# Storing a 128-row tile of the result as one transfer of two 64-row blocks, in a fused linear-attention and max-of-three feed-forward kernel

## The chip, the cores and the metric

The kernel runs on one core of one Trainium2 chip. A core has five engines with a queue of instructions each: TensorE (PE; its weight loads are listed apart as PEld), VectorE (DVE), ScalarE (ACT), GpSimd (POOL) and SyncE (SP), which here only issues transfers. Sixteen DMA engines carry the transfers that SP, ACT and POOL issue. The metric is the device time of one execution in microseconds (us); lower is better. Before the change the median of three runs was 283.24 us (282.25 to 283.63).

## What is computed

Batch 8, 8 heads, 576 tokens, head size 64. An attention with exponential features comes first; its output, 4608 rows of 512, goes through a feed-forward layer that takes the largest of three projections.

```python
def phi(x):
    proj = np.einsum('bhsd,df->bhsf', x, w_phi)             # 64 -> 128 features
    proj = proj - np.max(np.abs(proj), axis=-1, keepdims=True)
    return np.concatenate([np.exp(proj), np.exp(-proj)], axis=-1)
q_p, k_p = phi(q), phi(k)
kv = np.einsum('bhsf,bhsd->bhfd', k_p, v)
z = np.sum(k_p, axis=2)
num = np.einsum('bhsf,bhfd->bhsd', q_p, kv)
den = np.einsum('bhsf,bhf->bhs', q_p, z)[..., None] + 1e-06
x = (num / den)               # -> rows of (batch, token), 512 columns of (head, d)
h = np.maximum(np.maximum(x @ w1, x @ w2), x @ w3)          # 512 -> 768
out = h @ w_out                                             # 768 -> 512, float32
```

## The kernel before

**Tokens.** The 576 tokens of a head are loaded as 64 groups of nine (`c=NT`, `NT = 9`), so that 64 partitions hold one head and a partition reads 9 x 64 floats that lie together in DRAM. Token `9 i + c` is column `c` of partition `i`. Two heads share the 128 partitions. So in everything behind it the tokens of a batch stand in the order (c, i): first the 64 tokens with c = 0, then the 64 with c = 1, and so on.

**Units.** The attention works in 16 units (`attention`, four heads each, two units a batch): loads of q, k, v in float32 into `raw` buffers of 576 KB (eight of them); a cast to bf16 on POOL (`qk_bf`); a transpose to `qkT` (by TensorE for the first units, from unit 4 on by DMA on SP, L524); projections `psq` and `psk`; exponentials of k on ACT and maxima on DVE; the row maxima of q, turned on TensorE and put into row 64 of `qkT` by a transfer of 18 rows of 128 (`mT`, L582, on SP or ACT); the projections `psm` with their exponentials `Eq`; the products `kvps` and `psn`; and the division into `x_sb`. A second transpose by DMA on SP (`xT`, L703; by TensorE for the first two units) makes of `x_sb` the operand of the feed-forward layer.

**Chunks.** The feed-forward layer works in nine chunks (`chunk`). Chunk b = 0 to 7 holds the first 512 tokens of batch b in the order (c, i), that is c = 0 to 7; chunk 8 holds the tokens with c = 8 of all eight batches. A chunk multiplies by w2 - w1 and w3 - w1 (`ups`, L848), takes the maxima into `hT` on ACT and DVE, and adds x @ (w1 @ w_out) (L879) and `hT` @ w_out (L884) in PSUM. Chunks 0 to 4 copy each tile of 128 rows from PSUM to an `osb` buffer (four of them, `OSB`) and store it (L899). Chunks 5 to 8 (`FAST`) do this last product by Strassen's scheme of seven products of half size (`fast`, `fps`, L795), add up the tiles on DVE in two `raw` buffers, `low` and `high`, and store from there (L827).

**Stores.** A tile `tt` of a chunk b < 8 holds the 128 rows with c = 2 tt and c = 2 tt + 1. In the result, row `b * 576 + 9 i + c`, the 64 rows of one c stand 9 rows apart, and the two blocks of 64 start one row apart. `out_rows(tt)` gives a list of pairs (block of `out`, partitions of the tile), and the store issues one transfer for each. The chunk of the last tokens, b = 8, stores rows that stand 9 apart all through, in one transfer of 128 rows a tile, two tiles from SP and two from ACT.

**Order.** All instructions stand in a fixed order: `PLAN` lists each step with its engine, its start in the plan and its buffer, and every engine takes its steps in that order. SP's queue holds, mixed, the loads of `raw`, the transposes to `qkT` and `xT`, most of the `mT` transfers and all the stores of chunks 0 to 7. An engine waits at the step whose inputs or buffers aren't ready, with all that stands behind it. Transfers from SP and ACT take eight semaphores in turn; an issue waits until the transfer that last had its semaphore is done. The cost that a store has in the plan (`0.6 * n_out`) bears neither on the order, which `PLAN` fixes, nor on anything that is placed by it.

Of the kernel before, what the change touches and what calls it, by code (L numbers as in the profile page):

```python
# [19 lines left out]
P = 128  # L20
# [4 lines left out]
ST = S - SM  # L25
# [276 lines left out]
def kernel(  # L302
# [101 lines left out]
    def x_of(b):  # L404
        return xT[:, b % HELD]
# [311 lines left out]
    def t_nodes():  # L717
        for at, (n, c0) in enumerate(((2, 0), (2, 2), (1, 4))):
            def part(i, n=n, at=at):
                return t_end[:, i, :].unsqueeze(1) if at == 2 else xT[:, HELD + at, i, 0:DM].rearrange("p (c n) -> p c n", c=2)  # L720

            def quarter(r, w, n=n, c0=c0):
                m = slice(w * HF, (w + 1) * HF)
                return line_w[:, 2 * r:2 * r + 2, m] if c0 == 0 else wout_bf[:, 3 * r + c0 - 2:3 * r + c0 - 2 + n, m]
            pairs = [lambda q=quarter, p=part: (q(0, 1), q(0, 0)), lambda q=quarter, p=part: (q(1, 1), p(0)),
                     lambda q=quarter, p=part: (q(1, 1), q(0, 1)), lambda q=quarter, p=part: (q(1, 0), p(1))]
            need = [lines, [w_nodes[3]], [w_nodes[3]] + turned + diffs[0] + diffs[1]][at]
            made = []
            for i in range(4):
                def combine(i=i, pairs=pairs, part=part):  # L730
                    a, b = pairs[i]()
                    nc.gpsimd.tensor_tensor(part(i), a, b, ALU.subtract)
                n_ = node("tw", 0, {"POOL": 0.14 + 0.53 * n}, combine, need + [made[i - 1 - (i == 3)]] if i in (1, 3) else need, [])
                made.append(n_)
            t_made.extend(made)
# [220 lines left out]
    for b in range(B):  # L956
        if b == FAST[0]:
            t_nodes()
        rows = out[b * S:(b + 1) * S, :].rearrange("(i c) n -> c i n", c=NT)
        chunk(b, units[2 * b]["done"] + units[2 * b + 1]["done"], lambda ct, b=b: x_of(b)[:, ct, 0:SM],  # L960
              lambda ct, tt, b=b: x_of(b)[:, ct, tt * P:(tt + 1) * P],
              lambda tt, rows=rows: [(rows[2 * tt + i], slice(i * ST, (i + 1) * ST)) for i in range(2)], 2)
    lasts = []
    for b in range(B):
        lasts.append(node("C", 2 * b + 1, {"POOL": 0.4}, lambda b=b: nc.gpsimd.tensor_copy(
# [45 lines left out]
```

## Time and profile before

| | |
|---|---|
| median of 3 runs | 283.24 us |
| the profiled execution | 282.29 us |
| its span, first to last instruction | 280.5 us |
| granted TensorE clock, mean | 0.996 |
| HBM read and written | 34.64 MB and 9.44 MB |
| packets of DMA | 68050, of them 48746 under 512 B |

The span is shorter than the time by 1.8 us, which lie before the first and after the last instruction. A busy share is that of the whole span. The DMA rows give, for equal slices of the span or of a window, the busy share of the 16 DMA engines in tenths and the rate in GB/s. A row of a DMA queue has its number, kind, packets, MB, and the time that its packets took as a share of 16 engines in the window; q1 is SP's queue, q10 that of ACT. A row of the windows has the stretch in us, its length, the busy time of each engine with the count of its instructions, the granted clock, the share of DMA, and GB/s. In the chain of work that ended last, each row has a start, a duration and what held the path then. "SPq" is SP's sequencer: a row of it in the order of time has start, duration, line and transfer, and its durations are those of issuing, not of moving data.

### The profile page before, as it was taken

The page shows a single profiled execution, that of the slowest core. Times are in us where ns is not written, and L with a number is a line of the kernel's source. Part 1 is how long each engine was busy: PE and PEld are TensorE (multiplying, and loading weights), DVE is VectorE, ACT ScalarE, POOL GpSimd, SP SyncE. Part 2 cuts the span into 40 slices and gives each one's busy share as a digit, 9 for nine tenths or more (in the row PEclk, how much of TensorE's full clock was granted, in tenths as well). Part 3 has the DMA queues.
Part 4 walks back from the last instruction along what each step waited for, and adds up shares of the span by engine and source line. Part 5 has one row for each costly group of instructions (what it writes and reads, how often), then busy time and mean ns, then how long its engine had stood idle before and what let it go on. Part 6 is the DMA issues. An engine that isn't in the chain of part 4 may idle for free.

```text
span 280.5 us, 8829 instructions
## 1 busy us (share of the span) xinstructions
PE 270.9 (97%) x3663; PEld 164.1 (58%) x3663; DVE 224.0 (80%) x466; ACT 191.3 (68%) x439; POOL 168.5 (60%) x147
## 2 busy tenths in 40 slices
PE   8899999999999999999999999999999999999991
PEld 3566774465546555564556456565485589444881
DVE  4899899988869997889898878897589565756292
ACT  3799997798879988898684699887654860112000
POOL 8075787839444764570768079267875892927910
PEclk9999999999999999999999999999999999999998
DMA  7999999997999997799899729984232108245037
GB/s 212 234 211 320 266 224 197 384 277 139 287 382 245 197 313 251 193 204 227 240 263 156 194 49 261 202 201 89 51 78 49 40 18 118 55 95 116 0 89 212
DMA packets 68050, 51.46 MB, mean 183 GB/s; under 512 B 48746, under 2 KB 52650, under 8 KB 68010
## 3 DMA queue, kind: packets, MB, share of 16 engines
q1 hardware_dynamic: 63561, 45.41, 66.2%
q0 software_dynamic: 4000, 4.92, 10.3%
q8 instruction: 28, 0.46, 0.6%
q10 hardware_dynamic: 449, 0.57, 0.6%
q14 instruction: 12, 0.10, 0.1%
HBM read 34.64 MB, written 9.44 MB: 157 GB/s over the span
## 4 chain that ended last, share of the span: by engine, by line
PE 78%; DMA 9%; DVE 6%; ACT 3%; issue 1%; POOL 1%; DVEq 0%; POOLq 0%; ACTq 0%
PE ups L848 33%; PE fps L795 8%; PE ops L884 7%; PE psn L673 5%; PE kvps L655 5%; PE ops L879 5%; PE psq L547 5%; PE psm L626 5%; DMA qk_bf<-in_k_dram 3%; DMA qkT<-qk_bf 3%; DMA qkT<-mT 3%; ACT Eq L639 2%; DVE raw L802 2%; PE pm L950 2%; PE tps L509 1%; DVE mqp L566 1%
## 5 line engine op out<-in xcount | busy, mean ns | idle before, releaser
L601 POOL TENSOR_TENSOR vab<-raw,em 128x1152 bf16<-128x1152 f32 (+1 forms) x36 | 68.1, 1906 | 69.4 <-ACT em L597 55.1
L560 ACT ACTIVATE Ek<-psk 128x512 bf16<-128x512 f32 (+1 forms) x160 | 82.2, 568 | 13.8 <-PE psk L547 10.0
L848 PE MATMUL ups<-xT,w_bf 128*128 128x512 bf16 x384 | 90.8, 379 | 0.0
L639 ACT ACTIVATE Eq<-psm 128x512 bf16<-128x512 f32 (+1 forms) x160 | 79.4, 571 | 10.4 <-PE psm L626 9.6
L848 PEld LDWEIGHTS <-w_bf 128*128 128x128 bf16 x432 | 41.0, 98 | 46.4
L566 DVE TENSOR_REDUCE mqp<-psq 128x4 bf16<-128x512 f32 (+1 forms) x80 | 49.2, 634 | 8.4 <-PE psk L547 5.7
L566 DVE TENSOR_REDUCE mk<-psk 128x4 f32<-128x512 f32 (+1 forms) x80 | 48.9, 630 | 1.1 <-ACT Ek L560 0.5
L855 DVE TENSOR_TENSOR hT<-hT,ups 128x512 bf16<-128x512 bf16 x54 | 36.2, 684 | 16.8 <-PE ups L848 13.9
L857 ACT ACTIVATE hT<-ups 128x512 bf16<-128x512 f32 x28 | 16.6, 606 | 30.1 <-PE ups L848 30.0
L680 DVE TENSOR_TENSOR x_sb<-psn,rden 128x320 bf16<-128x320 f32 x64 | 31.5, 492 | 2.2
L492 POOL CAST qk_bf<-raw 128x1152 bf16<-128x1152 f32 x24 | 27.2, 1148 | 5.8 <-DMA qkT<-qk_bf 3.5
L673 PEld LDWEIGHTS <-Eq 128*128 128x128 bf16 x640 | 24.7, 97 | 7.5 <-ACT Eq L639 0.7
L884 PE MATMUL ops<-wout_bf,hT 128*128 128x512 bf16 x120 | 29.1, 379 | 0.0
L673 PE MATMUL psn<-kv_sb,Eq 128*128 128x65 bf16 x640 | 26.8, 194 | 0.5 <-ACT Eq L639 0.5
L547 PE MATMUL psq<-w,qkT 64*128 64x128 bf16 x288 | 24.5, 217 | 1.0 <-DMA qkT<-qk_bf 0.6
L547 PE MATMUL psk<-w,qkT 64*128 64x128 bf16 x288 | 24.1, 217 | 0.2
L547 PEld LDWEIGHTS <-qkT 64*128 64x128 bf16 x576 | 16.6, 94 | 12.7 <-issue 8.9
L626 PE MATMUL psm<-qkT,wphi_m 128*128 128x512 bf16 (+1 forms) x70 | 22.3, 359 | 0.5 <-DMA qkT<-mT 0.3
L879 PE MATMUL ops<-xT 128*128 128x512 bf16 x80 | 20.6, 380 | 0.0
L859 DVE TENSOR_SCALAR hT<-ups 128x512 bf16<-128x512 f32 x26 | 17.5, 684 | 3.8 <-PE ups L848 3.6
L655 PE MATMUL kvps<-vab,Ek 64*128 64x65 bf16 x1152 | 20.2, 190 | 0.0
L655 PEld LDWEIGHTS <-Ek 64*128 64x128 bf16 x1152 | 18.8, 94 | 2.3 <-DVE mk L566 0.4
(97 smaller groups left out, 333.8 us busy)
## 6 DMA issues: line engine op xcount, KB each, us to landing
raw<-in_v_dram SPq DMA_DIRECT2D x16, 576.0 KB
raw<-in_q_dram SPq DMA_DIRECT2D x12, 576.0 KB
raw<-in_k_dram SPq DMA_DIRECT2D x12, 576.0 KB
out_dram<-osb SPq DMA_DIRECT2D x40, 128.0 KB
out_dram<-raw SPq DMA_DIRECT2D x24, 128.0 KB
w_bf<-in_moe_w_dram POOLq DMA_DIRECT2D x3, 768.0 KB, 9.4
qk_bf<-in_q_dram POOLq DMA_DIRECT2D x3, 288.0 KB, 8.2
qk_bf<-in_k_dram POOLq DMA_DIRECT2D x3, 288.0 KB, 9.3
```

The lines of the kernel that those rows point to most:

```text
L547: nc.tensor.matmul(ps()[:, i, :], lhsT=cols[r, :], rhs=w2[r, c, :], start=True, stop=True)
L560: nc.scalar.activation(Ek[s]()[:, tiles_of(t0, n), :], of(1), EXP, scale=1.0 - 2.0 * s)
L566: nc.vector.tensor_reduce((mq, mk)[c]()[:, tiles_of(t0, n)], of(c), AXX, ALU.max, apply_absolute_value=True)
L601: (nc.vector if n_.eng == "DVE" else nc.gpsimd).tensor_tensor(vab()[:, g, t0:t1, 0:D], vb()[:, t0:t1, :], em()[:, g, t0:t1].unsqueeze(2).t ...
L626: nc.tensor.matmul(psm()[:, 0:w], lhsT=wphi_m, rhs=rhs, start=True, stop=True)
L639: nc.scalar.activation(Eqb()[s][:, cols], psm()[:, 0:w], EXP, scale=1.0 - 2.0 * s)
L655: nc.tensor.matmul(kvps[ab]()[:, t // NT, g, :], lhsT=Ek[g]()[r, t, :], rhs=vab()[r, g, t, :], start=(t + g == 0), stop=(t == UT - 1 and g ...
L673: nc.tensor.matmul(psn()[:, c, :], lhsT=Eqb()[g][:, t0:t0 + P], rhs=kv()[:, pr, ab, g, :], start=(g == 0), stop=(g == 1))
L848: nc.tensor.matmul(ups(), lhsT=w_bf[i + 1][:, ct, j * P:(j + 1) * P], rhs=tokens_of(ct), start=(ct == 0), stop=(ct == CT - 1))
L855: nc.vector.tensor_tensor(hT()[:, j, :], hT()[:, j, :], ups(), ALU.max)
L879: nc.tensor.matmul(ops_()[:, 0:width], lhsT=tile_of(ct, tt), rhs=line_w[:, ct, cols], start=(ct == 0), stop=False)
L884: nc.tensor.matmul(ops_()[:, 0:width], lhsT=hT()[:, j, tt * P:(tt + 1) * P], rhs=wout_bf[:, j, cols], start=False, stop=(j == JT - 1))
```

## The change

In `chunk` for batches 0 to 7, `out_rows` gives one pair in place of two: the blocks `2 tt` and `2 tt + 1` of the result together, an access of 2 x 64 x 512, for all 128 partitions of the tile. `n_out`, the number of transfers of a store, becomes 1. Chunk 8 is as it was.

```diff
         rows = out[b * S:(b + 1) * S, :].rearrange("(i c) n -> c i n", c=NT)
         chunk(b, units[2 * b]["done"] + units[2 * b + 1]["done"], lambda ct, b=b: x_of(b)[:, ct, 0:SM],
               lambda ct, tt, b=b: x_of(b)[:, ct, tt * P:(tt + 1) * P],
-              lambda tt, rows=rows: [(rows[2 * tt + i], slice(i * ST, (i + 1) * ST)) for i in range(2)], 2)
+              lambda tt, rows=rows: [(rows[2 * tt:2 * tt + 2], slice(0, P))], 1)
```

The order of instructions on TensorE, ACT, VectorE and POOL is the same. On SP each pair of stores becomes one. The first place is in the middle of the program, where three tiles of chunk 0 (`osb`) leave between a load and the transposes for later units; a row has the line, the operation, target and source, and the shape of the target.

```order
 L524 DMA_TRANSPOSE qkT<-qk_bf 128x18x128
 L486 DMA raw<-in_q_dram 128x2x576
-L899 DMA out_dram<-osb 64x512 x6
+L899 DMA out_dram<-osb 2x64x512 x3
 L524 DMA_TRANSPOSE qkT<-qk_bf 128x18x128
 L703 DMA_TRANSPOSE xT<-x_sb 128x10x128 x2
```

Six transfers of 64 rows became three of 2 x 64; the transposes behind them moved up by three places. The second place is the end of SP's queue, with the last tiles of chunk 4 and those of chunks 5 to 8.

```order
-L899 DMA out_dram<-osb 64x512 x2
+L899 DMA out_dram<-osb 2x64x512
 L703 DMA_TRANSPOSE xT<-x_sb 128x10x128
-L827 DMA out_dram<-raw 64x512 x2
+L827 DMA out_dram<-raw 2x64x512
 L703 DMA_TRANSPOSE xT<-x_sb 128x10x128
-L827 DMA out_dram<-raw 64x512 x22
+L827 DMA out_dram<-raw 2x64x512 x11
 L827 DMA out_dram<-raw 128x512 x2
```

There 26 issues became 14, and the last two, of chunk 8, are the same as before.

## The prediction

> **What bounds the kernel now.** I read the page first, for the busy shares and the chain of work that ended last.
>
> ```profile
> span 280.5 us, 8829 instructions
> PE 270.9 (97%) x3663; PEld 164.1 (58%) x3663; DVE 224.0 (80%) x466; ACT 191.3 (68%) x439; POOL 168.5 (60%) x147
> DMA  7999999997999997799899729984232108245037
> PE 78%; DMA 9%; DVE 6%; ACT 3%; issue 1%; POOL 1%; DVEq 0%; POOLq 0%; ACTq 0%
> ```
>
> TensorE is busy 97% of the span and holds 78% of the chain, so TensorE is the bound. But the DMA engines are busy at nine tenths for the first 60% of the span, and 9% of the chain is transfers. The chain in order of time shows which ones, and how the chunks of the second half follow one another:
>
> ```profile
> 51.41 5.36 DMA qkT<-mT
> ...
> 120.22 7.68 DMA qkT<-qk_bf
> ...
> 233.12 5.46 PE fps L795 x50
> 238.58 20.72 PE ups L848 x96
> 259.30 6.56 PE fps L795 x60
> ```
>
> At 120.22 us TensorE stood on the path behind a transpose by DMA for 7.7 us: the transfers of SP's queue have hardly any slack there. From 238.58 on TensorE runs alone to the end, and only stores are left on the queue.
>
> How a transfer is spread over the 16 engines is therefore what I looked at next, in two stretches of the DMA view: one with a single small transfer on ACT's queue (q10), and the last 40 us.
>
> ```profile
> core 0 of [0], span 280.5 us
> ...
> q10 hardware_dynamic: 27, 0.00, 0.5%
> ...
> qkT<-mT ACTq DMA_DIRECT2D x1, 4.5 KB
> ```
>
> ```profile
> GB/s 0 16 209 37 20 209 197 213 148 0 0 0 0 184 203 203 201 4 0 16 0 0 0 0 0 0 0 0 0 8 102 209 203 201 199 168 391 399 225 0
> DMA packets 2339, 3.97 MB, mean 99 GB/s; under 512 B 416, under 2 KB 416, under 8 KB 2336
> q1 hardware_dynamic: 2048, 3.41, 36.1%
> q10 hardware_dynamic: 288, 0.52, 3.4%
> ...
> out_dram<-raw SPq DMA_DIRECT2D x22, 128.0 KB
> out_dram<-raw ACTq DMA_DIRECT2D x2, 256.0 KB
> out_dram<-raw SPq DMA_DIRECT2D x2, 256.0 KB
> ```
>
> The packet counts tell how many engines a transfer used. On q10 in the last 40 us are two stores of 128 rows: 256 packets of data, and 32 more, 16 for each. On q1 are 22 stores of 64 rows and two of 128: 1408 + 256 packets of data, and 2048 - 1664 = 384 = 24 x 16 more. So each transfer ends with one small completion packet on every engine it used, and these used 16. The transfer of 18 rows (qkT<-mT, 18 pieces of 256 B) left 27 packets: 18 + 9. It used nine engines, the largest divisor of 18 up to 16. So the spread follows the shape of the transfer.
>
> **The change part by part.** The work on TensorE, ACT, VectorE and POOL stays as it was, in the same order. SP issues 32 transfers in place of 64, with the same bytes. What changes is their shape on the DRAM side: 64 x 512 before, 2 x 64 x 512 after, with the two blocks as the outermost dimension. The trace has no transfer whose outermost dimension is 2. By the row of 27 packets an outermost dimension of 18 went to nine engines; I take it that one of 2 goes to **two engines**, each with one block of 64 rows. The Trainium skill, in "DMA: Bandwidth & Descriptors", section "Why a DMA increments its semaphore by 16 and not by 1", states this as a rule: the number of engines is the largest one up to 16 that divides the slowest dimension over 1 of both access patterns. By that rule 18 gives nine, with which the trace agrees (27 packets), and 2 gives two, which no run here shows yet. Against the change it thus speaks for the whole loss below.
>
> *Price of a packet.* On q10 in the last 40 us: 3.4% of 16 engines x 40 us is 21.8 us for 256 packets of 2 KB, 85 ns each. On q1: 36.1% of 640 us is 231 us; less 256 x 85 ns it leaves 209 us for 1408 packets of the stores of 64 rows, 148 ns each. Before, a tile of 128 rows thus costs each of the 16 engines 8 x 148 ns = 1.18 us. After, it costs two engines 64 x p and the others nothing. For p the bounds are 85 ns (5.4 us a tile) and 148 ns (9.5 us). I take 85: the 148 comes where 16 engines share the rows of 64 partitions (about 205 GB/s in the row of GB/s, against 391 to 399 with 128 partitions), and two engines with 64 partitions each do not press on each other so. Each tile adds 5.4 - 1.2 = 4.2 us of work to those two engines.
>
> *The stretch of the middle.* All loads, transposes and stores of SP stand in one queue (q1), and loads and transposes use all 16 engines, so each waits for what stands ahead of it on the two loaded ones. The first store is issued at 73.78 us, and the last stretch of stores begins at 240.79:
>
> ```profile
> 73.78 1.19 SPq L899 DMA_DIRECT2D out_dram<-osb  x2
> ...
> 240.79 35.05 SPq L827 DMA_DIRECT2D out_dram<-raw  x24
> ```
>
> ```profile
> 73.80:240.80 167.00, 166.10 (x2290) 99.44 (x2288) 137.59 (x290) 125.32 (x288) 101.92 (x83) 1.00 0.76 176
> ```
>
> ```profile
> DMA packets 47029, 29.39 MB, mean 176 GB/s; under 512 B 38136, under 2 KB 38136, under 8 KB 47004
> ...
> out_dram<-osb SPq DMA_DIRECT2D x40, 128.0 KB
> ```
>
> Between them the engines were busy 0.76 x 167 = 127 us each. The 40 stores of osb are 20 tiles, and two of raw (issued at 231) one more: 21 x 4.2 = 88 us more on the two engines, 215 us of work for 167 us, **+48 us**. The lower bound goes by the best rate of the rows (399 GB/s): 29.39 MB take 74 us on each engine; less the stores at that rate (21 x 8 x 85 ns = 14 us), plus 21 x 5.4 = 113, it is 173 us, +6 us with the two engines never idle; nothing at all if loads, issued early, hide it. The upper bound, at 148 ns: 127 + 21 x 8.3 = 301 us, +134. I take +48. The share of 0.76 holds waits of packets for one another, which makes it too large; that the two engines also idle while SP waits for a tile makes it too small. TensorE cannot run ahead to cover this: each unit needs three of these transfers one after the other (transpose, mT, transpose of x_sb), and four stores in a row now stand for 4 x 5.4 = 22 us ahead of them. So the delay goes to the chain, where the wait of 7.68 us stands.
>
> *The end.* The row of GB/s (one slice a microsecond) shows the last 11 tiles come in three groups: four from 242 us on (1.03 MB), three from 253, four from 269. Before, each group drains before the next. After, the two engines need 22 us for the first (to 264), 16 for the second (to 280) and 22 for the third (to 302), without a pause. The four tiles of the last batch, unchanged, queue behind with eight packets each: 4 x 8 x 85 ns = 2.7 us, to 305. Now the traffic ends at 278.7 and the span at 280.5, so 1.8 us follow: 306.5, which is **+26 us** against 280.5. The delay of the middle moves all of this alike, and the two add.
>
> *SP's own time.* 32 issues go:
>
> ```profile
> L899 SPq DMA_DIRECT2D out_dram<-osb x40: 467/589/1467, 73.8 to 220.8; - x40
> ```
>
> At a median of 589 ns that is 19 us of SP's sequencer. I cost it at nothing, since SP waits longer than that for tiles:
>
> ```profile
> SPq L827 <- DVE raw L802: 25.9, 7, 13.3
> SPq L486 <- DVE raw L484: 22.4, 2, 16.0
> SPq L703 <- DVE mqp L566: 17.3, 5, 11.0
> ```
>
> *The sum.* 280.5 + 48 + 26 = 354.5 us of span. The profiled execution took 282.29 us, 1.8 more than its span, and the median of the three runs is 283.24, 1.0 above that one. 354.5 + 1.8 + 1.0 = 357.3. I say **357 us**.
>
> **The rivals.**
>
> *Still 16 engines.* The 18 rows of qkT<-mT stand first on both sides, so the row of 27 packets would also be met if the spread follows the rows of SBUF or the count of rows. Then 128 gives 16, and a tile costs 8 x 85 ns in place of 8 x 148, 0.5 us less an engine. In the middle TensorE is the bound and no store is on the chain. At the end, four tiles ahead of the last four are 2 us shorter, but the last stores are issued only when VectorE is done:
>
> ```profile
> L827 SPq DMA_DIRECT2D out_dram<-raw x26: 466/594/702, 231.1 to 275.4; - x26
> ```
>
> The last issue at 275.4 leaves at most some 1.5 us to gain before 278.7. Time: 282 to 283 us, no change or a little faster. The same time follows if the transfer is split back into two on its way to the chip. The Trainium skill, in the same page, "Rules for kernel authors", advises this edit: two transfers to disjoint halves of the partitions share the engines, use one of 128 partitions. The row of 205 against 399 GB/s bears out that 128 partitions drain faster, and by that rule alone the result would be this rival's. Chance 0.14.
>
> *Two engines, but the middle hides it.* Loads run up to several units ahead (eight raw buffers), so the 48 us might go into slack. For it: after 60% of the span the DMA row falls to 2 to 4 tenths. Against it: the transposes have no lead. Then only the end counts: 306.5 + 1.8 + 1.0 = 309 us. Chance 0.08.
>
> *Two engines at 148 ns a packet.* +134 in the middle, and at the end 242 + 11 x 9.5 + 2.7 + 1.8 = 351, +70: 487 us. Chance 0.05.
>
> **How the numbers follow.** My forecast has 0.73, the rivals 0.14, 0.08 and 0.05. The faster side is the first rival alone, and it ends there only if the end gains over 1.4 us (0.5% of 283, about what a measurement of this kernel can tell from no change): faster 0.04, same 0.10, slower 0.86. The forecast's own spread comes from the middle, +6 to +134 as the bounds have it; a packet at 100 ns in place of 85 would add 64 x 15 ns = 1 us to each of 32 tiles, 31 us. So I set the range from 300 to 400, which takes in the rival in which only the end counts; left out are no change and 487 us, with 0.19, and what little of the forecast's own case lies outside.
>
> **What would show it.** Packets on q1 over the whole execution: 63561 before. With two engines a tile leaves 128 + 2 packets in place of 2 x (64 + 16), so 32 x 30 = 960 fewer, 62601; with 16 engines it is 32 x 16 = 512 fewer, 63049.
>
> ```profile
> q1 hardware_dynamic: 63561, 45.41, 66.2%
> ```
>
> In the last 40 us the rate should fall to about 48 GB/s (two engines, 2 KB in 85 ns each) while stores alone run; the chain should show transfers, with qkT and xT waited for by TensorE far longer than 7.7 us, and at its end a DMA wait of over 20 us after the last addition on VectorE. The middle is right if the up projections of the last chunks start near 286 in place of 238.58. The forecast is wrong if q1 loses 512 packets, or if the store's packets take 148 ns on two engines as well.

## The result, and the profile after

| | before | after |
|---|---|---|
| median | 283.38 us (4 runs) | 378.85 us (4 runs, 377.93 to 379.67) |
| ratio, 95% interval | | 1.338 [1.333, 1.343] |
| span of the profiled execution | 280.5 us | 376.4 us |
| TensorE clock granted, mean | 0.996 | 0.891 |

The kernel became a third slower: 95.5 us between the medians. These lines of the page after the change answer to those shown of before; the two rows of tenths are the granted TensorE clock and the busy share of the DMA engines, in 40 slices.

```profile
span 376.4 us, 8753 instructions
PE 287.3 (76%) x3629; PEld 169.9 (45%) x3663; DVE 225.9 (60%) x466; ACT 192.8 (51%) x439; POOL 168.4 (45%) x147
PEclk9999999999786969879965789996999998999755
DMA  8999997999199949684298148895021271111221
q1 hardware_dynamic: 62601, 45.41, 56.5%
PE 43%; DMA 34%; SPq 4%; DVE 4%; ACT 3%; POOL 3%; issue 2%; DVEq 0%; ACTq 0%; POOLq 0%
```

The bytes on q1 are the same, 45.41 MB. Its packets are 62601, exactly the 960 fewer that two engines a store were to leave. DMA went from 9% to 34% of the chain that ended last, TensorE from 97% to 76% of the span, and over long stretches the DMA engines read one or two tenths, which is about what two of 16 make.

The last 40 us show that most plainly. This is the DMA view of that window, 1 us a slice:

```profile
GB/s 53 49 53 49 51 51 51 51 51 51 49 53 49 53 49 33 49 53 49 66 238 293 68 39 41 47 51 51 51 115 363 133 53 49 53 49 53 49 10 0
q1 hardware_dynamic: 1168, 2.30, 15.2%
q10 hardware_dynamic: 288, 0.52, 4.3%
```

Where stores of two blocks run alone the rate is 49 to 53 GB/s. Two engines with a packet of 2 KB in 85 ns each make 48. The two humps are the four transfers of chunk 8, which still use all 16 (on ACT's queue 288 packets, 144 for each of two).

The chain in order of time (start, duration, holder) has these pieces among others:

```profile
75.08 10.73 DMA qkT<-mT
...
91.37 8.76 DMA out_dram<-osb
...
145.95 13.38 DMA qkT<-qk_bf
186.00 13.87 DMA qkT<-qk_bf
...
310.83 12.42 PE ups L848 x49
...
332.06 18.50 DMA out_dram<-raw
...
355.38 0.60 DVEq L1006
```

The transposes to `qkT`, 7.7 us on the chain at worst before, now hold it for over 13. The up projections of the last chunks start at 310.83 where they started at 238.58, 72.3 us later. From there to the end of the span it is 65.6 us where it was 41.9: 23.7 us more. The last addition on VectorE ends at 355.4 us, 21 us before the end of the span, and stores fill most of that.

Of all transfers the small ones of `mT`, 18 rows each, hold the chain longest: 43 us in all, where they held it for 7.5. Those to `qkT` hold it for 27 us (7.7 before), those to `xT` for 12 (none before). At 91.37 us ACT waits for a store to give back an `osb` buffer, a wait that the forecast didn't have. TensorE's own waits for the first two kinds (total, times, longest, in us) were 0.3 and 0.6 us in total before, and are now:

```profile
PE psm L626 <- DMA qkT<-mT: 24.8, 7, 7.9
PE psq L547 <- DMA qkT<-qk_bf: 21.1, 3, 10.2
```

The longest of them, 10.2 us up to 199.92, shows what it waits for. This is the rate of all the DMA engines from 190 to 198 us, 0.2 us a slice:

```profile
GB/s 61 59 110 134 159 169 132 125 97 51 51 51 51 51 51 51 51 51 51 51 51 51 51 51 51 51 51 41 44 58 58 46 46 58 58 33 33 221 293 288
```

For more than 5 us of it the rate stays near the 48 GB/s of two engines, and only then does it rise again.

The windows up to the last up projections tell the 72.3 us apart (the second number is the length, the third TensorE's busy time; at the end of a row the granted clock, the share of DMA, and GB/s). First before, then after:

```profile
0.00:238.58 238.58, 234.91 (x3428) 141.16 (x3429) 200.32 (x430) 186.06 (x430) 147.35 (x132) 1.00 0.85 199
```

```profile
0.00:310.83 310.83, 248.47 (x3396) 146.19 (x3430) 204.55 (x433) 187.51 (x430) 147.28 (x131) 0.91 0.75 153
```

TensorE stands still for 62.4 us in place of 3.7, which is 58.7 of the 72.3. The other 13.6 us are the same matmuls taking longer: the granted clock is 0.91 in place of 1.00. This split is rough, since 34 of the 3663 records of matmuls are missing from the trace after the change. The run with the change in the middle alone (below) has them all, and up to its last up projections, at 308.44 us, it reads:

```profile
0.00:308.00 308.00, 250.70 (x3425) 145.61 (x3426) 201.97 (x429) 187.53 (x430) 147.18 (x131) 0.91 0.76 154
```

There TensorE stands still for 57.3 us, and its matmuls take 15.8 us longer than before.

### The profile page after: what moved, and what is told of

Same layout as the page of the kernel before. It is cut to its first block, busy times and chain, and to the rows that moved or that the text cites. A ratio compares the mean times of both kernels' runs of the same rounds, so it can differ in the third digit from the quotient of the medians.

```text
span 376.4 us, 8753 instructions
## 1 busy us (share of the span) xinstructions
PE 287.3 (76%) x3629; PEld 169.9 (45%) x3663; DVE 225.9 (60%) x466; ACT 192.8 (51%) x439; POOL 168.4 (45%) x147
## 3 DMA queue, kind: packets, MB, share of 16 engines
q1 hardware_dynamic: 62601, 45.41, 56.5%
## 4 chain that ended last, share of the span: by engine, by line
PE 43%; DMA 34%; SPq 4%; DVE 4%; ACT 3%; POOL 3%; issue 2%; DVEq 0%; ACTq 0%; POOLq 0%
PE ups L848 18%; DMA qkT<-mT 11%; DMA qkT<-qk_bf 7%; DMA out_dram<-raw 5%; PE ops L884 4%; DMA qk_bf<-in_k_dram 4%; PE kvps L655 3%; PE ops L879 3%; DMA xT<-x_sb 3%; PE psm L626 3%; PE psq L547 3%; PE psn L673 3%; DMA out_dram<-osb 2%; SPq L524 2%; PE fps L795 2%
## 5 line engine op out<-in xcount | busy, mean ns | idle before, releaser
L848 PE MATMUL ups<-xT,w_bf 128*128 128x512 bf16 x368 | 94.9, 394 | 5.7 <-DMA xT<-x_sb 4.5
L848 PEld LDWEIGHTS <-w_bf 128*128 128x128 bf16 x432 | 42.5, 101 | 55.8 <-issue 11.5
L547 PE MATMUL psq<-w,qkT 64*128 64x128 bf16 x288 | 26.8, 229 | 25.6 <-DMA qkT<-qk_bf 21.1
L626 PE MATMUL psm<-qkT,wphi_m 128*128 128x512 bf16 (+1 forms) x70 | 24.2, 387 | 24.8 <-DMA qkT<-mT 24.8
L547 PEld LDWEIGHTS <-qkT 64*128 64x128 bf16 x576 | 18.1, 99 | 38.6 <-DMA qkT<-qk_bf 22.0
L884 PE MATMUL ops<-wout_bf,hT 128*128 128x512 bf16 x114 | 31.7, 417 | 0.5 <-issue 0.3
L547 PE MATMUL psk<-w,qkT 64*128 64x128 bf16 x288 | 26.4, 229 | 0.2
L879 PE MATMUL ops<-xT 128*128 128x512 bf16 x70 | 22.5, 421 | 1.0 <-issue 0.7
L626 PEld LDWEIGHTS <-wphi_m 128*128 128x128 bf16 x70 | 6.6, 101 | 32.5 <-DMA qkT<-mT 26.5
```

The lines of the kernel that those rows point to most:

```text
L547: nc.tensor.matmul(ps()[:, i, :], lhsT=cols[r, :], rhs=w2[r, c, :], start=True, stop=True)
L626: nc.tensor.matmul(psm()[:, 0:w], lhsT=wphi_m, rhs=rhs, start=True, stop=True)
L848: nc.tensor.matmul(ups(), lhsT=w_bf[i + 1][:, ct, j * P:(j + 1) * P], rhs=tokens_of(ct), start=(ct == 0), stop=(ct == CT - 1))
L879: nc.tensor.matmul(ops_()[:, 0:width], lhsT=tile_of(ct, tt), rhs=line_w[:, ct, cols], start=(ct == 0), stop=False)
L884: nc.tensor.matmul(ops_()[:, 0:width], lhsT=hT()[:, j, tt * P:(tt + 1) * P], rhs=wout_bf[:, j, cols], start=False, stop=(j == JT - 1))
```

## Experiments

### One transfer of 128 rows on 16, 8 and 4 engines

The theory (A) is that a first dimension of 2 leaves the store two engines. The rival (B) is that one transfer of 256 KB costs the time whatever engines carry it, since it holds SP's queue and a buffer in one piece. Three kernels keep the single transfer of 128 rows a tile and change only which rows of the result it goes to, and with that the first dimension of the pattern. The rows of a batch then come out in another order; the first of the three kernels also leaves 56 of the 576 rows of a batch unwritten and writes 56 others twice.

```diff
-              lambda tt, rows=rows: [(rows[2 * tt:2 * tt + 2], slice(0, P))], 1)
+              lambda tt, b=b: [(out[b * S:b * S + SM, :].rearrange("(r c) n -> c r n", c=4)[tt], slice(0, P))], 1)
```

> One transfer of 128 rows a tile as in the change, but the 128 rows stand 4 apart in the result, so the pattern has 128 as its first dimension (the rows of a batch land in another order; the same bytes are stored). Theory A (the time comes from the two engines that a first dimension of 2 leaves): 16 engines, q1 with 63561 - 32 x 16 = 63049 packets, 281 to 284 us. Rival B (the time comes from the one larger transfer: 256 KB hold SP's queue and a buffer in one piece): about 379 us, as with the change.

```diff
-              lambda tt, rows=rows: [(rows[2 * tt:2 * tt + 2], slice(0, P))], 1)
+              lambda tt, rows=rows: [(rows[0:8, tt * 16:tt * 16 + 16], slice(0, P))], 1)
```

> As the change, but a tile goes to eight blocks of 16 rows, first dimension 8 (rows in another order, the same bytes). Theory A: eight engines, q1 with 63561 - 32 x 24 = 62793 packets, 16 x 85 ns = 1.4 us a tile where it was 1.2: 282 to 286 us. Rival B: about 379 us.

```diff
-              lambda tt, rows=rows: [(rows[2 * tt:2 * tt + 2], slice(0, P))], 1)
+              lambda tt, rows=rows: [(rows[tt // 2 * 4:tt // 2 * 4 + 4, tt % 2 * 32:tt % 2 * 32 + 32], slice(0, P))], 1)
```

> As the change, but a tile goes to four blocks of 32 rows, first dimension 4 (rows in another order, the same bytes). Theory A: four engines, q1 with 63561 - 32 x 28 = 62665 packets; a tile is 32 x 85 ns = 2.7 us on each of them, 1.5 more than before, so 21 tiles bring 32 us into a stretch of 167 us that held 127: still under it, and at the end the last group of four takes 10.9 us in place of 4.7; 284 to 300 us. Rival B (size of the transfer): about 379 us.

| first dimension | packets on q1 | median, us | ratio to before, 95% interval |
|---|---|---|---|
| 128 | 63049 | 283.19 | 0.999 [0.996, 1.002] |
| 8 | 62793 | 290.19 | 1.027 [1.020, 1.034] |
| 4 | 62665 | 322.54 | 1.139 [1.134, 1.144] |
| 2 (the change) | 62601 | 378.85 | 1.338 [1.333, 1.343] |

The counts of packets are those worked out, to the last one, and the time falls with the number of engines until with 16 nothing is left of the loss. The rates go with it: where stores run alone near the end, the DMA view shows about 385 GB/s with 16 engines, 195 with 8, 100 with 4 and 51 with 2. B is out. This also shows what the edit is worth by itself: with 32 issues fewer and 128 partitions a transfer, but on 16 engines, the interval takes in no change.

The sizes for 8 and 4 were too low. With eight engines the packets alone left 0.2 us more a tile; 290 us is above the 286 expected. With four, the sum of the work stayed under the length of the stretch, and the time still rose by 39 us. The row of the chain at which the last up projections start in the run with four engines:

```profile
273.20 20.45 PE ups L848 x94
```

That is 34.6 us later than before. So the middle loses time although the sum finds room for the work. The likely reason, which this run doesn't isolate, is that a transfer that TensorE awaits is late when a store stands ahead of it at that moment, however much time the engines have on average.

### The whole computation on 16 engines

The tile's tokens can be put in an order that suits one transfer: if c = 2 tt and 2 tt + 1 alternate, the pattern is 64 x 2 x 512.

```diff
-                    nc.scalar.activation(Eqb()[s][:, cols], psm()[:, 0:w], EXP, scale=1.0 - 2.0 * s)
+                    to, of_ = Eqb()[s][:, cols], psm()[:, 0:w]
+                    if w == SM:
+                        to = to.rearrange("p (t i c) -> p t c i", c=2, i=ST)
+                        of_ = of_.rearrange("p (t c i) -> p t c i", c=2, i=ST)
+                    nc.scalar.activation(to, of_, EXP, scale=1.0 - 2.0 * s)
...
-              lambda tt, rows=rows: [(rows[2 * tt:2 * tt + 2], slice(0, P))], 1)
+              lambda tt, b=b: [(out[b * S:(b + 1) * S, :].rearrange("(i c) n -> i c n", c=NT)[:, 2 * tt:2 * tt + 2, :], slice(0, P))], 1)
```

> The whole computation, with one transfer of 128 rows a tile on 16 engines: ACT writes the exponentials of q so that the tokens of c = 2 tt and 2 tt + 1 alternate, a tile then holds rows (i, c), and the DRAM pattern is 64 x 2 x 512. Theory A: 16 engines, q1 63049 packets, 281 to 284 us, if the writes of ACT at every second element cost nothing (160 of them at 571 ns before); up to 290 us if they take a tenth longer. Rival B: about 379 us.

287.03 us, ratio 1.012 [1.009, 1.015], with 63049 packets on q1. The stores are cured. What is left is put down to ACT, whose writes are the only other thing that the edit changes. Its exponentials of q in this run, with the duration's minimum, median and maximum in ns:

```profile
L643 ACT ACTIVATE Eq<-psm x160: 368/766/1178, 14.1 to 234.9; 128x512 bf16<-128x512 f32 x128, 128x256 bf16<-128x256 f32 x32
```

The median was 601 before, and ACT's busy time rose from 191.3 to 202.8 us. No version here beats the kernel before.

### The middle and the end apart

The change in chunks 0 to 4 alone, and in chunks 5 to 7 alone:

```diff
-              lambda tt, rows=rows: [(rows[2 * tt:2 * tt + 2], slice(0, P))], 1)
+              (lambda tt, rows=rows: [(rows[2 * tt:2 * tt + 2], slice(0, P))]) if b not in FAST else
+              (lambda tt, rows=rows: [(rows[2 * tt + i], slice(i * ST, (i + 1) * ST)) for i in range(2)]), 1)
```

> The change in chunks 0 to 4 alone (the 20 stores of osb); chunks 5 to 7 store in 64 rows as before. If the loss is the sum of two parts that lie in different stretches, as forecast, this run has the middle without the end. The forecast's middle gives 283 + 48 = 331 us; the trace of the change has the last up projections 72 us late, which gives 355 us. If the stores of chunks 5 to 7 are what holds the middle up, under 310 us.

The second has `if b in FAST`.

> The change in chunks 5 to 7 alone (the 12 stores of raw); chunks 0 to 4 store as before. Forecast: 26 us at the end and nothing in the middle, 309 us; from the trace of the change (24 us behind the last up projections) 307 us. With the run of the middle alone the two differences should add up to the 95 us of the whole change; if they add up to much less or more, the two parts act on one another.

The middle alone took 352.45 us, 1.246 [1.239, 1.254] times before, 69.3 us more. The end alone took 309.08 us, 1.091 [1.086, 1.096], 25.9 us more. Together that is 95.2 of the 95.5 us: the two parts add, as forecast. In the run of the end alone, the chain shows a buffer as well:

```profile
243.62 13.52 PE ups L848 x54
...
264.55 18.82 DMA out_dram<-raw
```

ACT stands idle for the last 11.6 of these 18.8 us, until a store gives back the `raw` buffer that chunk 8 writes next. The forecast didn't have this wait. It probably adds little of its own: all through it the stores go on at 49 to 53 GB/s, and they end last.

The same run shows what a single store does. Until 242.58 us only one store on two engines is issued, at 232.86. The transpose to `xT` behind it is issued at 235.69 and holds the chain for 7.89 us, and the last up projections start 5.0 us later than before the change.

### Two small transfers on two engines

```diff
-              lambda tt, rows=rows: [(rows[2 * tt:2 * tt + 2], slice(0, P))], 1)
+              lambda tt, rows=rows: [(rows[2 * tt:2 * tt + 2, i * 32:i * 32 + 32], slice(i * ST, (i + 1) * ST)) for i in range(2)], 2)
```

> Two transfers a tile as before the change, of 64 partitions each, but each to two blocks of 32 rows (2 x 32 x 512), so that each has 2 as its first dimension (rows in another order, the same bytes). Theory A (the work on the two engines): each tile brings them the same 64 packets, 370 to 385 us, q1 with 63561 - 64 x 14 = 62665 packets. Rival B (one transfer of 256 KB in one piece is the cost): 64 transfers of 128 KB, well under, 283 to 330 us.

383.56 us, ratio 1.356 [1.350, 1.362], and 62665 packets on q1. With transfers as small and as many as before the change, the loss is all there, and 5 us more. So it does not come from the size of a transfer.

### The stores in another queue

SP's transposes stand behind the stores in one queue. To see how much that order costs, the stores of chunks 0 to 7 go to ACT's queue, once as in the change and once, as a control, in 64 rows as before it.

```diff
         n.eng, n.start = {"T": "PE", "D": "DVE", "A": "ACT", "G": "POOL", "S": "SP"}[what[at]], float(start)
-        n.end = n.start + n.costs[n.eng] + LATENCY[n.eng]
+        if n.kind == "store" and n.u < B:
+            n.eng = "ACT"
+        n.end = n.start + n.costs.get(n.eng, 0.6) + LATENCY[n.eng]
```

> The change, with the stores of chunks 0 to 7 issued by ACT in place of SP, so that they stand in q10 and not in q1 with the loads and transposes. Theory C (the middle is lost because transposes and mT wait in one queue behind whole stores on the two engines): the two engines serve both queues, the middle loss falls to under half, 310 to 340 us. Theory D (the middle is lost because the two engines have too much work in all, in whatever order): as with the change, 370 us or more.

> Control for the run with the stores on ACT: stores of 64 rows on 16 engines as before the change, issued by ACT. What ACT's issues cost by themselves: 64 issues of some 0.4 us on an engine that is busy 68% of the span; 283 to 290 us by both theories.

373.62 us, ratio 1.316 [1.312, 1.321], against 290.25 us, 1.022 [1.018, 1.027], for the control, a little above the 283 to 290 expected of it. Beside its control the run loses 83 us, where the change lost 95 beside its own. So taking the stores out of SP's queue saves some 12 us, and theory C falls. The 12 us are no clean price of the order, since ACT now stands at a store's issue for up to 7.2 us (2.6 at most in the control), and part of what was saved may be lost there. SP's transposes to `qkT`, before, in the change, and with the stores on ACT (time of the issue in ns: minimum, median, maximum):

```profile
L524 SPq DMA_TRANSPOSE qkT<-qk_bf x12: 2711/3358/6156, 39.8 to 194.0; - x12
```

```profile
L524 SPq DMA_TRANSPOSE qkT<-qk_bf x12: 2434/6310/15432, 40.2 to 259.4; - x12
```

```profile
L526 SPq DMA_TRANSPOSE qkT<-qk_bf x12: 2638/4956/13217, 40.6 to 250.0; - x12
```

With the change SP stays at one issue for up to 15.4 us, and all behind it on SP waits too. With the stores in another queue the longest is still 13.2. That SP stands there until the two engines take more fits this, but no run shows it by itself.

### TensorE kept at work in its stalls

```diff
                 def proj(t0=t0, n=n, psq=psq, psk=psk):
+                    for _ in range({(8, 9): 14, (7, 4): 16, (10, 9): 22, (11, 4): 36}.get((u, t0), 0)):
+                        nc.tensor.matmul(psq().rearrange("p a d -> p (a d)"), lhsT=idle, rhs=idle.unsqueeze(1).to_broadcast([P, 4, P]), start=True, stop=True)
...
-            def mm(ts=ts, ch=ch, w=w, psm=psm):
+            def mm(ts=ts, ch=ch, w=w, psm=psm, hd=hd):
+                for _ in range({(8, 2): 18, (13, 2): 22, (12, 1): 28, (11, 1): 7, (14, 3): 7}.get((u, hd), 0)):
+                    nc.tensor.matmul(psm(), lhsT=idle, rhs=idle.unsqueeze(1).to_broadcast([P, 4, P]), start=True, stop=True)
```

> The change, with 170 idle matmuls of 512 columns (their product is thrown away) put ahead of the nine instructions before which TensorE stood longest in the trace of the change (46.7 us in all), sized to 80% of each stall: 170 x 0.216 = 37 us. They can only fill stalls. Theory E (part of the middle is lost because TensorE's granted clock, 0.91 up to the last chunk, falls in and after stalls and its own work then takes 13.6 us longer): the clock stays near 1 and the time falls by 5 to 15 us, to 364 to 374. Theory F (the clock costs nothing, since the next transfer is awaited anyway): 377 to 383 us.

373.47 us, ratio 1.318 [1.312, 1.323], which lies clear of the change's 1.338 [1.333, 1.343]. The window up to the last up projections:

```profile
0.00:306.57 306.57, 276.60 (x3565) 159.04 (x3600) 203.71 (x432) 186.88 (x430) 147.21 (x131) 0.98 0.77 155
```

The clock in it is 0.98 in place of 0.91, and the time is 5.4 us less although TensorE was given some 37 us of idle work more (170 matmuls of 0.216 us). So the clock costs at least some 5 us on the path; theory E holds, at the low end of what it expected.

## Why the prediction was right, and where its size was off

*Two engines.* Right, to the packet: 62601 on q1. The 27 packets of the transfer of 18 rows told it, with the assumption that 2 behaves as 18 did. The rule in the Trainium skill, "DMA: Bandwidth & Descriptors", section "Why a DMA increments its semaphore by 16 and not by 1", said the same, and the runs agree with it at 128, 8, 4 and 2. The rival with 16 engines is out for the change. As a kernel of its own, with 128 rows at one distance, it came out at no change, 283.19 us against the 282 to 283 that the rival gave. The Trainium skill, "DMA: Bandwidth & Descriptors", section "Rules for kernel authors", advises one transfer of 128 partitions in place of two to disjoint halves. In that run it cost nothing and gained nothing that an interval of [0.996, 1.002] could show.

*85 ns a packet.* Right: 49 to 53 GB/s where the stores run alone, 48 forecast; that is 77 to 84 ns. The rival at 148 ns is out.

*The end, +26.* Right in its mechanism: the two engines drain the last tiles nearly without a pause, 23.7 us more in the trace of the change. That the kernel of its own gave +25.9 is in part luck: some 5 us of it lie ahead of the last up projections, behind the one store at 232.86, where the forecast had nothing for this run. *The two parts add.* Right: 95.2 of 95.5 us. The rival in which the middle hides its part is out with it.

*The middle, +48.* This term was too small: it measured 69.3 alone and 72.3 in the trace, and the last up projections began at 310.83 us where I wrote 286. It is nearly all of the 22 us by which 357 fell short of 378.85, and the range, which was set wide for this term, held. Two things were wrong with it. First, TensorE's own work: I took stalls as time lost only while they last, and the clock then made 14 to 16 us more of the same matmuls; the run with the idle matmuls gave 5.4 us back. Second, I set the work of 215 us against the 167 us of the stretch, with everything but the stores at its price of before: 127 - 21 x 1.2 = 102 us an engine. In the trace of the change the stretch between the first store and the last group is this:

```profile
74.36:309.90 235.54, 178.68 (x2257) 103.60 (x2279) 139.12 (x290) 126.98 (x288) 99.73 (x80) 0.88 0.67 125
```

0.67 x 235.5 is 158 us, the mean of 16 engines; the 21 stores are 113 us on two of them, 14 in that mean; 144 us are left for the rest, 42 more than the 102, for the same bytes. This can't be work of the two engines, since 113 and 144 are more than the 235.5 us of the stretch. Nor is the share a plain measure of work: from 189.70 to 199.90 us it reads 1.08, so the times of packets overlap. The 127 us that the sum began with came from the same share. And the run with four engines lost 39 us although its work fitted the stretch. Beyond what such a sum holds, TensorE waits for single transfers that are late, those of `mT` (24.8 us in all) and of `qkT` (21.1), and ACT for an `osb` buffer. How the rest of the 22 us is shared among them the runs don't tell apart.

## What to carry to other kernels

Look at the outermost dimension of both access patterns of a transfer before merging two transfers into one: count its packets in the profile, and what exceeds the rows of data is, in all these runs, the number of engines that it used. Here a store on two engines delayed the transposes and the small transfers behind it, so its price was paid where TensorE waited for something else. A sum of work against time came out too low for that price, with two engines and with four.

## What the runs showed of the hardware

The granted TensorE clock falls with stalls. These are the waits on the transposes to `qkT` in the trace of the change (total, times, longest, in us), a window of 10 us whose first 3.9 us are the end of the longest one, and the up projections of the whole execution (minimum, median and maximum in ns):

```profile
PEld L547 <- DMA qkT<-qk_bf: 22.0, 4, 10.3
```

```profile
196.00:206.00 10.00, 6.08 (x30) 2.60 (x31) 2.82 (x5) 2.30 (x5) 0.00 (x0) 0.52 0.80 182
```

```profile
L848 PE MATMUL ups<-xT,w_bf x368: 376/379/634, 41.3 to 326.5; 128*128 128x512 bf16 x184
```

The clock there is 0.52 (0.50 in the first 3 us behind the wait), and an up projection takes up to 634 ns where none took over 390 before. The Trainium skill states in "TensorE: Matmul & The Clock Gate", section "Part 1: The HAM clock gate", that after some 3.4 us without work the clock goes to half. The 0.52 agrees; I hadn't put it into the sum. With idle matmuls in nine of the stalls the clock up to the last up projections was 0.98 in place of 0.91.

ACT's exponentials slowed from 601 to 766 ns at the median when 128 of the 160 wrote every second element.
